# Strassen's seven products for the second expert layer's hidden units, in three blocks of tokens

## The chip, the cores and the metric

The kernel runs on one core of one Trainium2 chip. The metric is the device time of one execution in microseconds (us), as the median of several runs; the profile is a further execution with the hardware profiler on. The engines are PE (TensorE; PEld are its weight loads), DVE (VectorE), ACT (ScalarE), POOL (GpSimd) and SP (SyncE, which issues DMAs).

## The reference

Three layers follow one another. The first is an attention over 4 batches, 8 heads of 64, with 512 local tokens (a window of 32 to either side, and 32 global tokens) and 32 global ones that see everything. Its output is a matrix x of 2176 tokens by 512. Then come two expert layers:

```python
h = np.maximum(x @ w_in, 0.0)          # first layer: 512 -> 2048 -> 512
x = h * h @ w_out

logits = x @ w_gate                    # second layer: 8 experts, 512 -> 1024 -> 512
P = np.exp(logits - logits.max())
for _ in range(8):                     # Sinkhorn
    P /= P.sum(1, keepdims=True) + 1e-09
    P /= P.sum(0, keepdims=True) + 1e-09
    P *= N / E
for e in range(E):
    out += P[:, e:e + 1] * (np.maximum(x @ w1[e], 0.0) @ w2[e])
```

Everything has float32's precision; w_in and w_out arrive as float64.

## The kernel before

A product with float32's precision is made of three PE matmuls in the format float32r: each operand is held as a pair (hi, lo), and `split_terms` gives hi x hi, hi x lo and lo x hi. Making a pair takes a copy into hi (ACT or POOL) and a subtraction into lo (DVE or POOL).

The attention ends in `xh` and `xl`, the pairs of x with its 512 features in four chunks of 128 partitions and the 2176 tokens along the free axis. The expert layers then go unit by unit; a unit is 512 hidden units in four pieces of 128. The first layer has U1 = 4 units, the second 16 (two for each expert). For each unit the tokens come in five blocks of 4, 4, 3, 3 and 3 tiles of 128. For each block, `hidden` (products at L237) makes four pieces: 4 chunks x 3 terms = 12 matmuls, weights stationary, 512 or 384 tokens moving. `hidden_out` turns them into pairs; in the second layer by ACT's Relu from PSUM (L249) and a DVE subtraction that reads PSUM and the hi part (L250). Then the outputs (`products`, L860): in the second layer `second_out` has 12 matmuls for each tile of 128 tokens, hidden units stationary and 512 columns of w2 moving, and DVE adds the result, scaled by the gate's probability, to `acc` (L908).

The order of each engine's instructions is the order in which the program emits them. `step_side` and `step_gate`, called after each piece and each output, put in steps of the work beside: the weights of the next unit (loaded by SP, split by POOL for the second layer at L177 and L179, six slots of pieces), and the gate. The gate's logits come from `gate_block` (L784), with w_gate padded to 128 columns and held as pairs, during the second layer's first unit; `gate_turn` (L794) turns them. `sinkhorn` then does its eight iterations in steps, the sums over tokens by a float32 matmul with ones (L819). The first layer's result is split into `xh` and `xl` again at L878 and L879.

Of the kernel before, what the change touches and what calls it, by code (L numbers as in the profile page):

```python
# [9 lines left out]
F32 = mybir.dt.float32  # L10
# [19 lines left out]
def kernel(  # L30
# [38 lines left out]
    # tiles of the attention whose place weights take at its end  # L69
# [12 lines left out]

    def double_words(raw, k):
# [6 lines left out]
        t = cv.tile([P, 512], F32, tag=f"t{k}", name="t")  # L90
        top = cv.tile([P, 512], F32, tag=f"top{k}", name="top")
        low = cv.tile([P, 512], F32, tag=f"low{k}", name="low")
# [29 lines left out]
    U1 = F1 // (UF * P)  # L122
    UE = F2 // (UF * P)
    NU = U1 + E * UE
    # of each slot (hi, lo) of the first weights [d, (chunk, unit)] and of the second ones [unit, d]
# [12 lines left out]
    def piece_src(g):  # L138
        u, fc = divmod(g, UF)
        if u < U1:  # L140
            f0 = g * P
            return w_in.bitcast(U32)[:, 2 * f0 : 2 * (f0 + P)], w_out.bitcast(U32)[f0 : f0 + P, :]
        e, half = divmod(u - U1, UE)
        f0 = (half * UF + fc) * P
        return w1[e, :, f0 : f0 + P], w2[e, f0 : f0 + P, :]
# [3 lines left out]
    def load_part(g, part, r=None):  # L149
        if g >= NU * UF:  # L150
            return
        src = piece_src(g)[part]
        if r is None:
            r = stage.tile([P, 1024], F32, tag=f"r{part}", name="raw")
            r = r.bitcast(U32) if g < U1 * UF else r[:, 0:512]
# [9 lines left out]
    def take(g, part, k):  # L165
        """The first steps of a part of a piece, which don't need its slot."""
        if g < U1 * UF:
            taken[g, part] = yield from double_words(raw[g][part], k)

    def place(g, part, then=None):  # L170
        """The last steps, into the slot."""
        hi, lo = slots[g % NB][part]
        if g < U1 * UF:
            yield from split_words(hi, lo, *taken.pop((g, part)))
        else:
            src = raw[g][part]
            nc.gpsimd.tensor_scalar(out=hi, in0=src, scalar1=1.0, scalar2=0.0, op0=ALU.mult, op1=ALU.add)  # L177
            yield
            nc.gpsimd.tensor_tensor(out=lo, in0=src, in1=f32(hi), op=ALU.subtract)  # L179
            yield  # L180
        placed.add((g, part))
        (then or (lambda: load_part(g + 2, part)))()
# [58 lines left out]
    def hidden_out(g, ps, n, r, s, rest):  # L241
        hh, hl = (x[:, 0:n] for x in hid[g % UF])
        if g < U1 * UF:
            nc.scalar.activation(out=r, in_=ps, func=AF.Relu)  # L244
            nc.scalar.activation(out=s, in_=r, func=AF.Square)
            nc.vector.tensor_tensor(out=hh, in0=r, in1=r, op=ALU.mult)  # L246
            rest.tensor_tensor(out=hl, in0=s, in1=f32(hh), op=ALU.subtract)  # L247
        else:
            nc.scalar.activation(out=hh, in_=ps, func=AF.Relu)  # L249
            nc.vector.scalar_tensor_tensor(out=hl, in0=ps, scalar=0.0, in1=f32(hh), op0=ALU.max, op1=ALU.subtract)  # L250

    # ================= attention =================
    with ExitStack() as actx:
# [59 lines left out]
        def warm(k):  # L313
            """Products of zeros: they keep the tensor engine at its full clock until there is work without gaps."""
# [11 lines left out]
        # masks of the negated scores  # L326
# [24 lines left out]
        def evacuate(*jobs):  # L351
            """Splits of PSUM into (hi, lo) that the next step does."""
# [47 lines left out]
        def prep_edges(n):  # L400
# [8 lines left out]
            else:  # L409
                # The first block has no previous keys and the last no next ones: the mask covers what lies there.  # L410
# [10 lines left out]
        def prep_v(n):  # L421
# [9 lines left out]
            # As with the keys, the mask covers what lies beyond the ends.  # L431
# [11 lines left out]
        # global keys and queries of all batches: [2 heads x 64, (hi, lo), pair, (batch, position)]  # L443
# [8 lines left out]
        # -- local queries: half an item is a pair of heads by two blocks of 128 queries --  # L452
# [76 lines left out]
        # -- global queries: four heads of 32 queries stacked on the partitions --  # L529
# [36 lines left out]
        def glob_normalise(i):  # L566
            # The reciprocal sums wait for the products: a partition has one query here and there.
# [6 lines left out]
        def glob_transpose(i, n):  # L574
# [7 lines left out]
            # The global keys land on the partitions that vg has their values on.  # L582
# [5 lines left out]
        def glob_values(i, n):  # L588
# [6 lines left out]
            # each head's queries by the values of all four heads  # L595
# [56 lines left out]
        # Step k has the products of scores k and values k - 4 and the turning of probabilities k - 2, all of them  # L652
        # read from PSUM in the next step, where softmax k - 1 goes on too.
# [82 lines left out]
    psh = ctx.enter_context(tc.tile_pool(name="psh", bufs=3, space=PSUM))  # L736
    psy = ctx.enter_context(tc.tile_pool(name="psy", bufs=3, space=PSUM))
    psm = ctx.enter_context(tc.tile_pool(name="psm", bufs=2, space=PSUM))
# [7 lines left out]
    acc_d = acc.rearrange("p (c n) -> p c n", c=NC)  # L746
    acc_t = acc.rearrange("p (j d) -> p j d", d=DM)

# [10 lines left out]
    wg = {}  # L759
    ones = mp.tile([P, P], F32, name="ones")  # L760
    prob = mp.tile([P, NTILE, E], F32, name="prob")
    l2 = mp.tile([P, NTILE, 2 * E], F32, name="l2")
    mxb = mp.tile([P, P], F32, name="mxb")
    ss = mp.tile([P, 64], F32, name="ss")

    def gate_setup():
        wga = cv.tile([P, NC, P], F32R, tag="top0", name="wga")
        wgb = cv.tile([P, NC, P], F32R, tag="low0", name="wgb")
        wg[0] = wga, wgb
        nc.vector.memset(f32(wga), 0.0)  # L770
        nc.vector.memset(f32(wgb), 0.0)
        nc.vector.memset(ones, 1.0)
        nc.vector.tensor_copy(wga[:, :, 0:E], wgr)
        nc.vector.tensor_copy(wgb[:, :, 0:E], wgr)
        nc.vector.tensor_tensor(out=wga[:, :, E : 2 * E], in0=wgr, in1=f32(wga[:, :, 0:E]), op=ALU.subtract)

    def gate_block(tb):
        j0, nj = blocks[tb]
        c0, n = j0 * P, nj * P
        ps = psm.tile([P, 512], F32, tag="m", name="m")  # L780
        k = 0
        for c in range(NC):
            for w, x in zip(wg[0], (xh, xl)):
                nc.tensor.matmul(ps[:, 0:n], lhsT=w[:, c, :], rhs=x[:, c, c0 : c0 + n], start=(k == 0), stop=(k == 2 * NC - 1))  # L784
                k += 1
        lt = tp.tile([P, 512], F32, tag="r", name="lt")
        nc.scalar.copy(lt[0 : 2 * E, 0:n], ps[0 : 2 * E, 0:n])
        return lt

    def gate_turn(tb, lt):  # L790
        j0, nj = blocks[tb]
        ps = psm.tile([P, 4, 2 * E], F32, tag="m", name="m")
        for t in range(nj):
            nc.tensor.transpose(ps[:, t, :], lt[0 : 2 * E, t * P : (t + 1) * P], ident[0 : 2 * E, 0 : 2 * E])  # L794
        nc.scalar.copy(l2[:, j0 : j0 + nj, :], ps[:, 0:nj, :])

    def sinkhorn():
        nc.vector.tensor_tensor(out=prob, in0=l2[:, :, 0:E], in1=l2[:, :, E : 2 * E], op=ALU.add)
# [5 lines left out]
        ps = psm.tile([P, P], F32, tag="m", name="m")  # L804
# [6 lines left out]
        for _ in range(SINKHORN):  # L811
# [6 lines left out]
            ps = psm.tile([P, NTILE, E], F32, tag="m", name="m")  # L818
# [8 lines left out]

    def prepare(g):
# [157 lines left out]
```

## Time and profile before

| | |
|---|---|
| median of 3 runs | 2093.18 us (2092.74 to 2093.88) |
| span of the profiled execution | 2091.8 us |
| PE busy | 2066.2 us, 99%, 10549 matmuls |
| DVE, ACT, POOL busy | 817.5, 486.9, 467.3 us |
| mean granted TensorE clock | 0.994 of full speed |

The span runs from the first to the last instruction of the profiled execution; a run's time holds a little more than it. Busy time of an engine says how much of the span it had an instruction in work; which of its waits set the end is read from the chain of work that ended last, which is followed back from the last instruction.

### The profile page before, as it was taken

How to read it: one execution, taken by the hardware profiler on the slowest of the kernel's cores; microseconds unless marked ns; L12 is line 12 of the kernel's file. 1: busy time of each engine (PE TensorE's matmuls, PEld its weight loads, DVE VectorE, ACT ScalarE, POOL GpSimd, SP SyncE). 2: the span in 40 equal slices, each digit the busy share in tenths (PEclk: the TensorE clock that was granted, in tenths of full speed). 3: DMA queues.
4: the chain of work that ended last, by engine and by line, in shares of the span. 5: the costliest groups of instructions: out<-in, count | busy, mean ns of one | idle time of the engine just before them, and what ended most of it. 6: DMA issues, size and time to landing. Idle time of an engine off the chain costs nothing.

```text
span 2091.8 us, 26331 instructions
## 1 busy us (share of the span) xinstructions
PE 2066.2 (99%) x10549; PEld 1826.9 (87%) x10549; DVE 817.5 (39%) x1633; ACT 486.9 (23%) x1121; POOL 467.3 (22%) x567
## 2 busy tenths in 40 slices
PE   8998999999999999999999999999999999999999
PEld 7997798998989898888889898888889888888988
DVE  7999556656421343322222222222222222222222
ACT  6896442333322111101111011111111110111111
POOL 6556332315320211202020210202020220202000
PEclk8999999999999999999999999999999999999999
DMA  7664111111010101101010100101010110101011
GB/s 158 138 144 123 41 61 43 42 49 31 5 36 11 31 11 31 39 2 41 1 41 11 31 21 21 41 1 41 1 41 11 31 32 9 41 1 41 1 36 51
DMA packets 160730, 80.33 MB, mean 38 GB/s; under 512 B 95840, under 2 KB 148320, under 8 KB 160608
## 3 DMA queue, kind: packets, MB, share of 16 engines
q1 hardware_dynamic: 160608, 78.65, 14.1%
q8 instruction: 83, 1.36, 0.3%
q14 instruction: 39, 0.32, 0.1%
HBM read 63.72 MB, written 4.46 MB: 33 GB/s over the span
## 4 chain that ended last, share of the span: by engine, by line
PE 93%; DVE 4%; ACT 1%; issue 1%; DMA 1%; POOL 0%; SPq 0%; DVEq 0%; POOLq 0%; ACTq 0%
PE y L860 44%; PE h L237 44%; PE pv L524 1%; PE s L461 1%; PE pta L507 1%; DVE e L471 1%; DVE xl L363 0%; PE pv L602 0%; PE ptb L510 0%; PE s L548 0%; PE m L784 0%; DVE al L363 0%; DVE hid L246 0%; DVE bl L363 0%; DMA vb<-va 0%
## 5 line engine op out<-in xcount | busy, mean ns | idle before, releaser
L237 PE MATMUL h<-xh,w 128*128 128x384 f32 (+1 forms) x3200 | 901.6, 357 | 0.8 <-ACT rs L244 0.8
L860 PE MATMUL y<-w,hid 128*128 128x512 f32 x3276 | 755.8, 389 | 0.0
L860 PEld LDWEIGHTS y<-w,hid 128*128 128x128 f32 x3276 | 612.6, 188 | 124.7
L237 PEld LDWEIGHTS h<-xh,w 128*128 128x128 f32 x3200 | 588.4, 188 | 53.1 <-ACT rs L244 1.2
L237 PE MATMUL h<-xl,w 128*128 128x384 f32 (+1 forms) x1600 | 570.4, 356 | 0.0
L249 ACT ACTIVATE hid<-h 128x384 fp32r<-128x384 f32 (+1 forms) x320 | 171.1, 535 | 1266.7 <-PE h L237 1262.7
L250 DVE SCALAR_TENSOR_TENSOR hid<-h,hid 128x384 fp32r<-128x384 f32 (+1 forms) x320 | 195.5, 611 | 631.6 <-ACT hid L249 631.6
L908 DVE SCALAR_TENSOR_TENSOR acc<-y,prob,acc 128x512 f32<-128x512 f32 x239 | 174.3, 749 | 438.2 <-PE y L860 437.7
L177 POOL TENSOR_SCALAR w<-raw 128x512 fp32r<-128x512 f32 x128 | 81.2, 640 | 1175.3 <-PE h L237 1041.7
L237 PEld LDWEIGHTS h<-xl,w 128*128 128x128 f32 x1600 | 300.5, 188 | 26.4
L860 PE MATMUL y<-hid,w 128*128 128x384 f32 (+1 forms) x960 | 191.5, 357 | 4.4 <-DVE hid L247 2.2
L860 PEld LDWEIGHTS y<-hid,w 128*128 128x128 f32 x960 | 171.8, 188 | 21.3 <-DVE hid L247 3.4
L179 POOL TENSOR_TENSOR w<-raw,w 128x512 fp32r<-128x512 f32 x128 | 166.3, 1310 | 5.4
L113 POOL TENSOR_TENSOR top<-top,w 128x512 f32<-128x512 f32 x32 | 47.7, 1498 | 215.1 <-ACT w L111 155.6
L246 DVE TENSOR_TENSOR hid<-r 128x384 fp32r<-128x384 f32 (+1 forms) x76 | 53.8, 708 | 84.1 <-ACT r L244 84.0
L244 ACT ACTIVATE r<-h 128x384 f32<-128x384 f32 (+1 forms) x76 | 40.3, 531 | 140.9 <-PE h L237 139.4
L492 POOL TENSOR_SCALAR e<-e,st 128x224 f32<-128x224 f32 x128 | 55.5, 453 | 66.4 <-PE pta L581 26.1
L482 ACT ACTIVATE e<-e,st 128x224 f32<-128x224 f32 x128 | 60.1, 475 | 7.4 <-DVE st L471 7.3
L247 DVE TENSOR_TENSOR hid<-g,hid 128x384 fp32r<-128x384 f32 (+1 forms) x76 | 58.4, 768 | 7.9
L875 DVE TENSOR_TENSOR acc<-y,acc 128x384 f32<-128x384 f32 (+1 forms) x60 | 36.3, 608 | 49.8 <-PE y L860 49.8
L461 PE MATMUL s<-kt,q 64*128 64x224 f32 x384 | 43.4, 296 | 6.9 <-DVE st L471 2.9
L461 PEld LDWEIGHTS s<-kt,q 64*128 64x128 f32 x384 | 37.0, 195 | 12.2 <-DVE st L471 3.7
(152 smaller groups left out, 1160.6 us busy)
## 6 DMA issues: line engine op xcount, KB each, us to landing
raw<-in_moe_w_dram SPq DMA_DIRECT2D x128, 256.0 KB, 2.8
raw<-in_moe_w_in_dram SPq DMA_DIRECT2D x16, 512.0 KB, 3.8
raw<-in_moe_w_out_dram SPq DMA_DIRECT2D x16, 512.0 KB, 4.2
rqk<-in_k_l_dram SPq DMA_DIRECT2D x32, 128.0 KB, 2.6
rqk<-in_q_l_dram SPq DMA_DIRECT2D x32, 128.0 KB, 2.8
rv<-in_v_l_dram SPq DMA_DIRECT2D x32, 128.0 KB, 2.7
out_dram<-acc SPq DMA_DIRECT2D x15, 256.0 KB, 2.0
vb<-va SPq DMA_DIRECT2D x32, 112.0 KB, 3.2
```

Source lines behind the costliest of these rows:

```text
L177: nc.gpsimd.tensor_scalar(out=hi, in0=src, scalar1=1.0, scalar2=0.0, op0=ALU.mult, op1=ALU.add)
L179: nc.gpsimd.tensor_tensor(out=lo, in0=src, in1=f32(hi), op=ALU.subtract)
L237: nc.tensor.matmul(ps, lhsT=w, rhs=x, start=(k == 0), stop=(k == 3 * NC - 1))
L246: nc.vector.tensor_tensor(out=hh, in0=r, in1=r, op=ALU.mult)
L247: rest.tensor_tensor(out=hl, in0=s, in1=f32(hh), op=ALU.subtract)
L249: nc.scalar.activation(out=hh, in_=ps, func=AF.Relu)
L250: nc.vector.scalar_tensor_tensor(out=hl, in0=ps, scalar=0.0, in1=f32(hh), op0=ALU.max, op1=ALU.subtract)
L461: nc.tensor.matmul(s[:, t, :], lhsT=a, rhs=c, start=(x == 0), stop=(x == 2))
L482: nc.scalar.activation(out=v, in_=v, func=AF.Exp, bias=st[:, c : c + 1], scale=-1.0, accum_out=st[:, 4 + c : 5 + c])
L492: nc.gpsimd.tensor_scalar(out=v, in0=v, scalar1=st[:, 4 + c : 5 + c], scalar2=1.0, op0=ALU.mult, op1=ALU.mult)
L860: nc.tensor.matmul(ps, lhsT=w, rhs=m, start=(f == 0 and x == 0), stop=(f == last and x == 2))
L908: nc.vector.scalar_tensor_tensor(out=s, in0=ps, scalar=prob[:, j, e : e + 1], in1=s, op0=ALU.mult, op1=ALU.add)
```

## The change

The second layer's hidden products are done as one two-by-two block product in Strassen's form (Winograd's variant): tokens in two halves, features in two halves (A11, A12, A21, A22), and 256 hidden units in two halves of 128 (B11 to B22). Four sums of each side, S1 to S4 and T1 to T4, are made by POOL in float32 and then split into pairs; seven products of 6 matmuls each take the place of eight. The results come together partly in PSUM, where a product accumulates on another's bank, and partly by DVE additions with a copy of an intermediate result in SBUF (`snaps`).

The tokens go in three blocks TBS of 6, 6 and 5 tiles (halves of 384, 384 and 320 tokens), and the loop over them is now outside that over the 16 units: all w1 and w2 are loaded and split once per block. The forms of a block's tokens lie in `xh` and `xl`, the hidden units' pairs behind them. `step_side` no longer runs in the second layer; `hook` steps the gate and, in the outputs, four steps of the next unit's weights. The first layer's outputs stay float32 in `acc`; `gate_block` multiplies them with w_gate as plain float32, 4 matmuls of 8 columns per tile. PSUM has 2 x 2 + 1 banks for hidden products and 3 for outputs.

```diff
+    def form_sums(tb):
...
+        add = nc.gpsimd.tensor_tensor
+        add(out=s1, in0=a21, in1=a22, op=ALU.add)
+        yield
+        add(out=s2, in0=s1, in1=a11, op=ALU.subtract)
+        yield
+        add(out=s4, in0=a12, in1=s2, op=ALU.subtract)
+        yield
+        add(out=s3, in0=a11, in1=a21, op=ALU.subtract)
+        yield
+    def form_splits(tb):
...
+        for name in FORMS:
+            src = sums[tb][name]
+            hi, lo = token_form(name, n)
+            nc.scalar.copy(hi, src)
+            nc.vector.tensor_tensor(out=lo, in0=src, in1=f32(hi), op=ALU.subtract)
+            yield
+    def weight_splits(s, q, t, plain):
...
+        for c, k, src in srcs:
+            nc.scalar.copy(dst(0, c, k), src)
+            yield
+        for c, k, src in srcs:
+            nc.vector.tensor_tensor(out=dst(1, c, k), in0=src, in1=f32(dst(0, c, k)), op=ALU.subtract)
+            yield
+    def second_weights(s):
+        for q in range(2):
+            r = raw_pairs.pop((s, q, 1))
+            for i in range(2):
+                split_pool(*slots[2 * q + i][1], r[:, i])
+            load_pair_of_pieces(s + 1, q, 1)
+    PRODUCTS = {
+        1: ("A11", "B11"), 2: ("A12", "B21"), 3: ("S4", "B22"), 4: ("A22", "T4"),
+        5: ("S1", "T1"), 6: ("S2", "T2"), 7: ("S3", "T3"),
+    }
+    ORDER = ((1, 0), (5, 0), (2, 0), (1, 1), (5, 1), (6, 0), (2, 1), (6, 1), (3, 0), (7, 0), (3, 1), (7, 1), (4, 0), (4, 1))
+    def second_hidden(n, hook):
...
+        def hide(z, piece, half):
+            hh, hl = (x[:, half * n : (half + 1) * n] for x in hidden_of(piece, n))
+            nc.scalar.activation(out=hh, in_=z, func=AF.Relu)
+            late.append((z, hh, hl))
+        def flush():
+            for z, hh, hl in late:
+                nc.vector.scalar_tensor_tensor(out=hl, in0=z, scalar=0.0, in1=f32(hh), op0=ALU.max, op1=ALU.subtract)
+            late.clear()
+        def add(ps, snap, piece, half):
+            z = tp.tile([P, 512], F32, tag="rg"[count[0] % 2], name="z")[:, 0:n]
+            count[0] += 1
+            nc.vector.tensor_tensor(out=z, in0=ps, in1=snap, op=ALU.add)
+            flush()
+            hide(z, piece, half)
+        for i, q in ORDER:
+            if i == 1:
+                a[q] = psa.tile([P, 512], F32, tag="a", name="pa")[:, 0:n]
+                product(1, q, a[q], True)
+                nc.scalar.copy(p1, a[q])
...
+            elif i == 7:
+                product(7, q, a[q], False)
+                add(a[q], p5[q], 2 * q + 1, 1)
+            else:
+                product(4, q, a[q], False)
+                flush()
+                hide(a[q], 2 * q, 1)
+            hook()
+        flush()
+    for tb, (j0, nj) in enumerate(TBS):
+        n = nj * P // 2
+        for u in range(NS):
+            s = tb * NS + u
+            second_weights(s)
+            if u == NS // 2:
+                run(form_sums(tb + 1))
+            second_hidden(n, step_gate)
+            if tb == 0 and u == UE:
+                while gate:
+                    step_gate()
+            todo = []
+            if s + 1 < len(TBS) * NS:
+                todo.append(first_weights(s + 1, range(2)))
+            if u == NS - 1:
+                todo.insert(0, form_splits(tb + 1))
+            work = itertools.chain(*todo)
+            next(work, None)
+            def hook():
                 step_gate()
+                for _ in itertools.islice(work, 4):
+                    pass
...
+            for i, tile_ in enumerate(order):
+                second_out(tb, u, tile_, s == len(TBS) * NS - 1 and i == nj - 1, hook)
+            run(work)
```

`first_weights` makes the four T sums of both halves of a unit's weights (`weight_sums`, POOL, 256 elements a partition each) and then steps through `weight_splits`. In the last unit of the first layer the sums of block 0 are made on POOL, and its seven `form_splits` stand in the side work of the last `first_out`; `gate_block` for the last tokens follows it.

## Rows read from the trace of the kernel before

**Rows 1.** The page: busy time of each engine, and the granted clock in 40 slices.

```profile
PE 2066.2 (99%) x10549; PEld 1826.9 (87%) x10549; DVE 817.5 (39%) x1633; ACT 486.9 (23%) x1121; POOL 467.3 (22%) x567
...
PEclk8999999999999999999999999999999999999999
```

**Rows 2.** The page: the chain that ended last, by line.

```profile
PE y L860 44%; PE h L237 44%; PE pv L524 1%; PE s L461 1%; PE pta L507 1%; DVE e L471 1%; DVE xl L363 0%; PE pv L602 0%; PE ptb L510 0%; PE s L548 0%; PE m L784 0%; DVE al L363 0%; DVE hid L246 0%; DVE bl L363 0%; DMA vb<-va 0%
```

**Rows 3.** The chain in order of time through one unit of the second layer: start and length in us, what, and how many. Left out are the second block of 512 tokens, which is like the first, and the third of 384, which is like the second.

```profile
784.21 10.88 PE h L237 x48
795.09 10.88 PE y L860 x48
...
827.73 8.35 PE h L237 x48
836.07 8.20 PE y L860 x36
844.27 8.34 PE h L237 x48
...
877.37 2.72 PE h L237 x12
```

**Rows 4.** Busy time by stretch (PE, PEld, DVE, ACT, POOL, each with its count; granted clock, DMA share, GB/s).

```profile
784.00:2090.00 1306.00, 1304.60 (x6229) 1139.58 (x6228) 352.76 (x537) 149.68 (x280) 197.35 (x211) 1.00 0.08 24
```

**Rows 5.** PE in order of time, at 384 columns (three matmuls from 1499.72 to 1500.24) and at 256 (the values of the attention).

```profile
1499.72 0.51 PE L237 MATMUL h<-xh,w 128*128 128x384 f32 x2
...
1500.24 0.51 PE L237 MATMUL h<-xh,w 128*128 128x384 f32 x2
...
102.04 0.28 PE L524 MATMUL pv<-al,va 128*128 128x256 f32 x1
102.16 0.28 PE L524 MATMUL pv<-ah,va 128*128 128x256 f32 x1
```

**Rows 6.** The chain in order of time, the gate's pieces: a block of 512 tokens and its four turns, a block of 384 (there are two and three of them), and a sum of a Sinkhorn iteration.

```profile
596.35 1.81 PE m L784 x8
...
609.05 0.35 PE m L794 x4
...
642.10 1.39 PE m L784 x8
...
705.44 0.23 PE m L819 x2
```

**Rows 7.** Groups of instructions by line, shapes apart: count, busy us, mean ns of one, idle before.

```profile
L237 PEld LDWEIGHTS h<-xh,w 128*128 128x128 f32 x3200 | 588.4, 188 | 53.1 <-ACT rs L244 1.2
L250 DVE SCALAR_TENSOR_TENSOR hid<-h,hid 128x384 fp32r<-128x384 f32 x192 | 107.0, 557 | 334.7 <-ACT hid L249 334.7
L250 DVE SCALAR_TENSOR_TENSOR hid<-h,hid 128x512 fp32r<-128x512 f32 x128 | 88.5, 691 | 296.8 <-ACT hid L249 296.8
L875 DVE TENSOR_TENSOR acc<-y,acc 128x384 f32<-128x384 f32 x36 | 19.8, 555 | 29.1 <-PE y L860 29.1
L908 DVE SCALAR_TENSOR_TENSOR acc<-y,prob,acc 128x512 f32<-128x512 f32 x237 | 173.3, 751 | 436.6 <-PE y L860 436.0
L111 ACT CAST w<-top 128x512 fp32r<-128x512 f32 x32 | 19.0, 616 | 32.9 <-DVE top L102 19.8 <-PE y L860 13.1
```

**Rows 8.** DVE in order of time, the rows' part (4 operations from 701.33) and the columns' part (5 from 709.12) of one Sinkhorn iteration.

```profile
701.33 0.28 DVE L812 TENSOR_REDUCE ss<-prob 128x17 f32<-128x136 f32 x1
...
702.16 0.30 DVE L815 TENSOR_TENSOR prob<-prob,ss 128x136 f32<-128x136 f32 x1
...
709.12 0.29 DVE L821 TENSOR_REDUCE ss<-m 128x8 f32<-128x136 f32 x1
...
710.09 0.30 DVE L825 TENSOR_TENSOR prob<-prob,ss 128x136 f32<-128x136 f32 x1
```

**Rows 9.** In order of time, the end of a hidden piece: the first matmul of what follows on PE, and ACT's read of the piece.

```profile
2044.31 0.61 PE L860 MATMUL y<-w,hid 128*128 128x512 f32 x2
2044.51 0.60 ACT L249 ACTIVATE hid<-h 128x512 fp32r<-128x512 f32 x1 [2.12 <-PE h L237]
```

**Rows 10.** Durations of a line (minimum, median and maximum in ns; span of its starts in us; shapes), and DVE and POOL in order of time near 575 and 588 us.

```profile
L247 DVE TENSOR_TENSOR hid<-g,hid x76: 557/559/1607, 234.2 to 578.3; 128x384 fp32r<-128x384 f32 x48, 128x512 fp32r<-128x512 f32 x28
L250 DVE SCALAR_TENSOR_TENSOR hid<-h,hid x320: 550/558/693, 588.9 to 2080.8; 128x384 fp32r<-128x384 f32 x96, 128x512 fp32r<-128x512 f32 x64
...
574.58 1.46 DVE L247 TENSOR_TENSOR hid<-g,hid 128x384 fp32r<-128x384 f32 x1
576.61 0.56 DVE L247 TENSOR_TENSOR hid<-g,hid 128x384 fp32r<-128x384 f32 x1
...
574.15 1.47 POOL L179 TENSOR_TENSOR w<-raw,w 128x512 fp32r<-128x512 f32 x1
588.34 1.29 POOL L179 TENSOR_TENSOR w<-raw,w 128x512 fp32r<-128x512 f32 x1
588.86 0.69 DVE L250 SCALAR_TENSOR_TENSOR hid<-h,hid 128x512 fp32r<-128x512 f32 x1 [2.83 <-ACT hid L249]
```

**Rows 11.** Durations of POOL's lines, in the same form.

```profile
L177 POOL TENSOR_SCALAR w<-raw x128: 614/623/1172, 496.7 to 1995.3; 128x512 fp32r<-128x512 f32 x128
L179 POOL TENSOR_TENSOR w<-raw,w x128: 1281/1290/1740, 498.8 to 1996.0; 128x512 fp32r<-128x512 f32 x128
L879 POOL TENSOR_TENSOR xl<-acc,xh x20: 1010/1018/1297, 509.1 to 586.7; 128x384 fp32r<-128x384 f32 x12, 128x512 fp32r<-128x512 f32 x8
```

More of the change, by code (lines that the diff above doesn't have):

```diff
@@ L777, in gate_block @@
[L777 to L795, printed above, removed]
+    logits = []
+    def gate_block(b):
+        if not logits:
+            logits.append(psa.tile([P, NTILE, E], F32, tag="m", name="lg"))
+        for j in range(blocks[b][0], blocks[b][0] + blocks[b][1]):
+            tb = next(i for i, (j0, nj) in enumerate(TBS) if j0 <= j < j0 + nj)
+            t0 = (j - TBS[tb][0]) * P
+            for c in range(NC):
+                nc.tensor.matmul(
+                    logits[0][:, j, :], lhsT=first_outputs(tb)[:, c, t0 : t0 + P], rhs=wgr[:, c, :],
+                    start=(c == 0), stop=(c == NC - 1),
+                )
@@ L847, in hidden, with first_out @@
         hidden_out(g, ps, n, r, s, nc.vector)
-    def products(outs, n, terms):
-        tiles = [None] * len(outs)
+    def first_out(u, c0, n):
+        assert all((u * UF + i, 1) in placed for i in range(UF))
+        tiles = [None] * NC
         last = UF - 1
         order = [(0, f) for f in range(last)] + [(1, f) for f in range(last)] + [(0, last), (1, last)]
-        order += [(o, f) for o in range(2, len(outs)) for f in range(UF)]
-        for o, f in order:
+        order += [(d, f) for d in range(2, NC) for f in range(UF)]
+        for d, f in order:
@@ L882, in second_out @@
[L882 to L903 removed]
+            if f < last:
+                continue
@@ new lines, in form_splits @@
+    def form_splits(tb):
+        if tb >= len(TBS):
+            return
+        n = TBS[tb][1] * P // 2
+        for name in FORMS:
[4 more added lines that the diff above has]
+            yield
+    chunks = (
+        [slots[i][part][x] for i in (4, 5) for part in range(2) for x in range(2)],
+        [slots[i][0][x] for i in range(UF) for x in range(2)],
+    )
@@ new lines, in second_hidden, with product @@
+    def second_hidden(n, hook):
+        a, d, u2, p5 = {}, {}, {}, {}
+        p1 = snaps[:, 0, 0:n]
+        late = []
+        count = [0]
+        def product(i, q, ps, first):
+            x, w = (token_form(PRODUCTS[i][0], n), weight_form(q, PRODUCTS[i][1]))
+            t = 0
+            for k in range(2):
+                for lhs, rhs in split_terms(w[0][:, k], w[1][:, k], x[0][:, k], x[1][:, k]):
+                    nc.tensor.matmul(ps, lhsT=lhs, rhs=rhs, start=(first and t == 0), stop=(t == 5), skip_group_check=True)
+                    t += 1
+        def hide(z, piece, half):
[17 more added lines that the diff above has]
+                nc.scalar.copy(p1, a[q])
+            elif i == 5:
+                d[q] = psa.tile([P, 512], F32, tag="m", name="pd")[:, 0:n]
+                product(5, q, d[q], True)
+                p5[q] = snaps[:, 1 + q, 0:n]
+                nc.scalar.copy(p5[q], d[q])
+            elif i == 2:
+                b = psb.tile([P, 512], F32, tag="b", name="pb")[:, 0:n]
+                product(2, q, b, True)
+                add(b, p1, 2 * q, 0)
+            elif i == 6:
+                product(6, q, a[q], False)
+                u2[q] = snaps[:, 3 + q, 0:n]
+                nc.scalar.copy(u2[q], a[q])
+            elif i == 3:
+                product(3, q, d[q], False)
+                add(d[q], u2[q], 2 * q + 1, 0)
+            elif i == 7:
+                product(7, q, a[q], False)
+                add(a[q], p5[q], 2 * q + 1, 1)
+            else:
+                product(4, q, a[q], False)
[3 more added lines that the diff above has]
+        flush()
@@ new lines, in second_out @@
+    def second_out(tb, u, tile, split, hook):
+        j0, nj = TBS[tb]
+        e, half = divmod(u, UE)
+        j = j0 + tile
+        for d0, dn in ((0, DM // 2), (DM // 2, DM // 2)) if split else ((0, DM),):
+            d = slice(d0, d0 + dn)
+            ps = psy.tile([P, 512], F32, tag="y", name="y")[:, 0:dn]
+            t = 0
+            for f in range(UF):
+                hh, hl = (x[:, tile * P : (tile + 1) * P] for x in hidden_of(f, nj * P // 2))
+                wh, wl = (x[:, d] for x in slots[f][1])
+                for lhs, rhs in split_terms(hh, hl, wh, wl):
+                    nc.tensor.matmul(ps, lhsT=lhs, rhs=rhs, start=(t == 0), stop=(t == 3 * UF - 1))
+                    t += 1
+            hook()
+            s, pr = acc_t[:, j, d], prob[:, j, e : e + 1]
+            if u == 0:
+                if tb == 0:
+                    nc.scalar.copy(s, ps)
+                else:
+                    nc.scalar.activation(out=s, in_=ps, func=AF.Copy, scale=pr)
+            elif e == 0 and tb == 0:
@@ L937 @@
                 step_side(5 if opens else 2)
+                if u == U1 - 1 and tb and fc == 1:
+                    gate_block(tb - 1)
             if u == 0 and tb == 0:
@@ L941 @@
                 prepare(UF)
-            if u == U1:
-                lt = gate_block(tb)
-            if u < U1:
-                first_out(u, c0, n)
-            else:
-                second_out(u, tb, u == NU - 1 and last)
-            if u == U1:
-                gate_turn(tb, lt)
+            if u == U1 - 1 and last:
+                side.append((None, form_splits(0)))
+                step_side(2)
+            first_out(u, c0, n)
+            if u == U1 - 1 and tb == 1:
+                side.append((None, form_sums(0)))
         closed.clear()
@@ L952, with first_weights @@
             step_side(1)
-        if u == U1 + UE - 1:
-            while gate:
-                step_gate()
+    tw = share.tile([P, 2, 4, 2, P], F32, tag="va0", name="tw")
+    snaps = share.tile([P, 5, NH], F32, tag="va1", name="snaps")
+    def first_weights(s, qs):
+        for q in qs:
+            run(weight_sums(s, q, tw[:, q]))
+        for q in qs:
+            for plain in (True, False):
+                yield from weight_splits(s, q, tw[:, q], plain)
+            raw_pairs.pop((s, q, 0))
+            load_pair_of_pieces(s + 1, q, 0)
+    raw_pairs.pop((0, 0, 0))
+    load_pair_of_pieces(1, 0, 0)
+    run(first_weights(0, (1,)))
+    gate_block(len(blocks) - 1)
+    gate.append(sinkhorn())
+    NS = E * UE
+    for tb, (j0, nj) in enumerate(TBS):
+        n = nj * P // 2
[16 more added lines that the diff above has]
+            def hook():
+                step_gate()
+                for _ in itertools.islice(work, 4):
+                    pass
+            order = list(range(nj))
+            if tb == len(TBS) - 1 and u == NS - 1:
+                order = [0, 1, nj - 1, *range(2, nj - 1)]
+            for i, tile_ in enumerate(order):
+                second_out(tb, u, tile_, s == len(TBS) * NS - 1 and i == nj - 1, hook)
+            run(work)
 _INS = ['q_l', 'k_l', 'v_l', 'q_g', 'k_g', 'v_g', 'moe_w_in', 'moe_w_out', 'moe2_w_gate', 'moe2_w1', 'moe2_w2']
```

219 lines of the change are left out of this document (113 added, 106 removed).

## The prediction

> **What bounds the kernel now.** I read the page's busy shares and slices first [rows 1], then the chain that ended last [rows 2], then that chain in order of time through one unit of the second layer [rows 3]. PE is busy 99% of the span at full granted clock, and 44% of the chain is the hidden products (L237), 44% the output products (L860). In the unit from 784.21 to 877.37 us the chain is nothing but blocks of 48 and 36 matmuls end to end. So time is PE's column count, plus a fixed part per matmul, plus whatever new wait the change puts in PE's way. The other engines have room on average: between 784 and 2090 us DVE is busy 353 of 1306 us and POOL 197 [rows 4].
>
> **Part 1, seven products for eight.** What one matmul takes is read from start to start. At 512 columns it is 10.88 / 48 = 226.7 ns [rows 3], at 384 columns 0.52 / 3 = 173.3 ns, at 256 columns 120 ns [rows 5]. The three lie on one line: columns / 2.4 GHz plus 13.3 ns. The 256-column row also shows that weight loads don't bind down to 120 ns, so 320 columns are put at 133.3 + 13.3 = 146.7 ns.
>
> Before, one unit's hidden products take 2 x 10.88 + 8.35 + 2 x 8.34 = 46.79 us [rows 3]. After, a unit is done three times, each with 14 products of 6 matmuls: 84 x 173.3 ns = 14.56 us for the two blocks of six tiles (384 columns), 84 x 146.7 ns = 12.32 us for the block of five (320 columns), 41.44 us together. That is 5.35 us less for each of 16 units: **-85.6 us**. The output products stay: 17 tiles of 12 matmuls at 512 columns, 16.3 us for six tiles and 13.6 us for five. The two ends are close here: by columns alone it would be 87, by [rows 3] and the line 85.6.
>
> **Part 2, the gate.** Removed: 40 matmuls with xh and xl, 2 x 1.81 + 3 x 1.39 = 7.8 us, and 17 turns at 0.35 / 4 us, 1.5 us [rows 6]. Added: 17 tiles x 4 chunks in plain float32. The matmul with the ones (L819) is plain float32, and [rows 6] has two instructions for each of its calls, 0.23 us for both at 136 columns; so 136 instructions here, with 8 columns each. The nearest rows are 87.5 ns for one turn of 16 columns (0.35 / 4) and 115 ns for L819. I take 100 ns, 13.6 us; the far end is a weight load of 188 ns that nothing covers [rows 7], 25.6 us. Net **+4.3 us**, from +2.6 to +16.3.
>
> **Part 3, into the second layer.** The first layer's last unit used to run straight on. Now DVE must do seven form_splits of 768 elements inside the last first_out: at 0.557 us for 384 elements and 0.691 for 512 (L250, [rows 7]) 1.04 ns for each further one, so 0.95 us each, 6.7 us, with four additions of 0.55 us (L875) among them in queue order, 2.2 us. DVE comes free from the last hidden units about 2 us into first_out, so the last addition ends at about 11 us, where PE is through after 8.3 us. gate_block(4) waits for it. **+2.7 us**, from 0 (PE's other work fills it) to 6 (POOL's sums hold DVE up too).
>
> **Part 4, the sinkhorn steps.** They were one step in each hidden() and output, which come 2.7 us apart; now it is one in each product, 1.04 us apart. One iteration's nine DVE operations take 1.1 + 1.3 us [rows 8], and it has four steps, 4.2 us of products. DVE has 14 operations of 0.555 us in 14.6 us of products already, so 2.2 us in those four. 4.6 us of DVE in 4.2 us of PE, and PE's matmul with the ones stands two products behind the rows' division in PE's queue: everything behind it waits. About six of the eight iterations fall into products: some 1.3 us each, **+8 us**, from 0 to 20.
>
> **Part 5, the steady unit: DVE's burst at the end of the products.** PE's wait is product 14, which accumulates into the bank that product 12's addition reads. The products 9 to 12 all end in an addition from PSUM (0.555 us, as L875 for 384), and each addition is followed by a subtraction for the hidden unit before (0.557 us). Count from the end of product 9: its result is there 0.2 us later (the 48th matmul of a hidden unit gives way to the next at 2044.31, ACT reads at 2044.51 [rows 9]). Undisturbed, DVE ends product 12's addition at 0.2 + 3 x 1.11 + 0.555 = 4.09 us, and product 14 is due at 4 x 1.04 = 4.16 us. It just fits; with 320 columns (0.49 us an operation, 0.88 us a product) it is 0.2 + 3 x 0.98 + 0.49 = 3.63 against 3.52 us, 0.1 us late.
>
> But the subtraction changes its kind. Today's (L250) reads PSUM and takes 550 to 693 ns whatever POOL does. The new one reads two SBUF tensors, as L247 does: 557 ns at best, up to 1607 [rows 10]. The rows of time there show why: the L247 that began at 574.58 took 1.46 us beside POOL's L179 of 574.15, and the next one 0.56 us at 576.61 with no POOL operation beside it, while L250 took 0.69 us at 588.86 inside POOL's L179 of 588.34. What is POOL doing then? After each unit's last output tile it splits four w2 pieces, 4 x (0.62 + 1.29) = 7.7 us, beginning some 2 us before the tile ends; then eight weight_sums of 256 elements, 1.29 - 2 x 0.275 = 0.74 us each (the step of 0.275 per 128 elements from L879's 1.015 and L179's 1.29, [rows 11]), until about 12 us into the products, or 13 with DVE's share. The burst is from 9.4 to 13.5 us. Each subtraction then finds POOL's operation begun 0.555 us before, with 0.19 us to go: two or three such waits, and a first one of up to 0.74, put the addition 0.3 to 1.3 us behind. I take 0.45 us for each of 48 units, **+21.6 us**. Ends: 0 (the sums are over by then) and 3 x 0.74 = 2.2 us each, 106 us, if every subtraction waits for a whole operation.
>
> The Trainium skill says of this (page "SBUF — State Buffer", section "Who interferes with whom") that a DVE instruction with two SBUF inputs and a GpSimd instruction that reads SBUF exclude one another, whoever comes second being blocked until the first is through. By it every subtraction could lose a whole POOL operation, which is the far end above; the row of 574.58 agrees in kind (1.04 us of overlap with POOL's operation cost it 0.9 us).
>
> The rest of a unit is covered. w2's splits (7.7 us) are due only at the first output tile, 12 to 14 us into the unit. The weight splits, 7 x 0.69 us of DVE and 7 x 0.62 us of ACT (L111, [rows 7]), stand beside 16.3 us of output products with 6 x 0.75 us of accumulations (L908): 9.3 us of DVE and a backlog of 1 to 2. POOL's 13.6 us lie in 31 us. If that cover went, the 4.8 us of weight splits would be late for the next product 1. SP's loads, now 48 units of four transfers, run on at about 3 x 24 GB/s [rows 4]; each is asked for most of a unit before its use.
>
> **Part 6, between blocks.** Twice, form_sums puts 4 operations of 768 elements (1.84 us) into POOL's queue ahead of the sums, in the burst; and twice form_splits adds 6.7 us of DVE to an output stage, 6.7 + 4.5 + 4.8 + 2 of backlog = 18 us beside 16.3. About 1 us for each of the four: **+4 us**, from 0 to 10.
>
> **The sum.** -85.6 + 4.3 + 2.7 + 8 + 21.6 + 4 = -45.0 us. On the profiled span, 2091.8 - 45.0 = 2046.8 us. The runs' median is 2093.18, 1.4 us above that span, for what lies around it; so **2048 us**.
>
> **Rivals.** *All hidden.* If the sums are through before product 9 and the sinkhorn waits fall into slack, parts 3 to 6 cost 0 to 15 us: 2093.2 - 85.6 + 4.3 = 2012, up to 2027. For it: POOL has only 7.7 + 5.9 us of work per unit and could start early. Against it: DVE's burst leaves 0.07 us even undisturbed, and at 320 columns nothing.
>
> *Slower: the lock in the burst.* DVE's subtractions lose a whole POOL operation each in products 9 to 12, and product 14 stands still. Price 48 x 2.2 us = 106 us, so 2093.2 - 85.6 + 15 + 106 = 2129 us. It decides from (85.6 - 15) / 48 = 1.5 us a unit on. For it: L247's maximum is 1607 ns, 1.0 us above its best, and if the w2 splits (1.29 us each) slide into the burst the waits are that long. Against it: the addition between two subtractions needs no port, and POOL's operation runs out meanwhile.
>
> *A halved version.* Part 5 at about 1.1 us, with the gate's far end: -85.6 + 16 + 53 + 10 = -7, 2086 us.
>
> **Chances.** The forecast, with 2028 to 2070 as its own range, 0.60. All hidden 0.18. The halved version, 2070 to 2089, 0.09. No change to 0.2% (2089 to 2097), which is about what a measurement of this kernel tells from none, 0.03. Slower 0.10. The range from 2015 to 2083 leaves out a third of the all-hidden case, a third of the halved one, and all above: about 2 in 10. Faster: 0.60 + 0.18 + 0.09 = 0.87.
>
> **What would show it.** Right: in the chain L237's successor takes 14.56 us in 84 matmuls with 384 columns and 12.3 with 320, and the output products 16.3 and 13.6; among the waits, PE on DVE's addition once per unit near half a microsecond, in front of the last product; DVE's subtraction of hidden units with a mean well above 0.56 us and a maximum over 1 us; gate instructions near 100 ns. Wrong: PE idle between all products (an ordering of reads and writes within xh and xl that I took to be fine), weight loads that stretch the 320-column matmuls past 150 ns, or a wait for weights at product 1.

## The result and the profile after

The changed kernel takes 2040.91 us (median of 4 runs, 2036.57 to 2044.99) where the kernel before takes 2093.46 beside it: a ratio of 0.9749, 95% interval 0.9732 to 0.9766. The forecast was 2048 in a range from 2015 to 2083. The profiled run took 2037.85 us with a span of 2035.9, so 55.9 us less than the span of [rows 1]; the forecast for it was 45.0 less. The sum came near, but its terms did not: one of 21.6 us was not there, and others were missing.

The page after, which answers to [rows 1] (busy time, granted clock) and to [rows 2] (the chain by line):

```profile
PE 1997.6 (98%) x10820; PEld 1814.2 (89%) x10820; DVE 1210.8 (59%) x2398; ACT 807.9 (40%) x1856; POOL 922.6 (45%) x1071
...
PEclk8999999999989999999999999999999999999999
...
PE y L1050 36%; PE pa L987 18%; PE pd L987 9%; PE y L854 8%; PE h L246 8%; PE pb L987 5%; DVE e L476 1%; PE pv L529 1%; DVE xl L368 1%; DVE xl L997 1%; DVE al L368 1%; PE lg L783 1%; DVE z L1003 1%; DVE bl L368 1%; PE s L466 1%
```

PE is still the chain, in the seven products (L987, by the banks pa, pd and pb) and the outputs (L1050). DVE and POOL have become half busy. The slice from 560 to 611 us has a granted clock of 0.8 to 0.9, which before has nowhere past the start.

The chain in order of time, which answers to [rows 3]: a steady unit of 384 columns, the start of the next, one of 320 columns (the start of its products, and its outputs), and unit 8 of the first block.

```profile
696.15 16.36 PE y L1050 x72
712.51 1.06 PE pa L987 x6
713.58 1.04 PE pd L987 x6
...
723.98 3.12 PE pa L987 x18
727.10 16.36 PE y L1050 x72
...
1772.23 0.88 PE pa L987 x6
1773.11 0.88 PE pd L987 x6
...
1810.67 13.62 PE y L1050 x60
1836.70 13.62 PE y L1050 x60
...
874.65 0.56 DVE z L1003
875.21 1.48 DVE xl L997
...
877.80 1.65 DVE xl L997
...
879.93 1.64 DVE xl L997
...
883.09 1.75 PE pa L987 x6
884.85 17.48 PE y L1050 x72
```

Products take 1.04 and 0.88 us each, 14 of them 14.59 us (712.51 to 727.10), and the unit 30.95 (26.03 with 320 columns), without a gap. In unit 8 the chain leaves PE for DVE's subtractions (L997), three of which take 1.5 to 1.7 us in place of 0.47.

From such rows the 55.9 us come apart as follows. Units: 2 x 30.95 + 26.03 = 87.93 us for 93.16 before, 16 times, -83.7. Gate: 112 instructions in 12.2 us are 109 ns each, 136 of them 14.8 us for 9.3 before, +5.5. Clock: stretches at the lower level after gate blocks and behind unit 8, 1.6 + 1.7 + 0.8 + 2.7 + 1.1, +7.9 (the one at 621 is counted with the Sinkhorn steps). Wait for the last addition ahead of the last gate block: +1.0. Sinkhorn steps: 5.6 us in the products of unit 0 (22.82 less 14.59 and the clock's 2.7), 6.0 in those of unit 1 (20.56 less 14.59) and 0.2 for a sum in the outputs, less the eight sums of 0.23 that stood on PE's chain before [rows 6], together +10. The two units 8 and the block change: 3.0 + 1.5 + 0.4, +4.9. That is -54.4; the other 1.5 us lie in the two kernels' starts and ends.

The granted clock was the surprise. Windows of the changed kernel: busy time of PE, PEld, DVE, ACT and POOL with counts, granted clock, DMA share and GB/s.

```profile
518.00:522.00 4.00, 4.00 (x36) 3.88 (x34) 1.53 (x3) 1.23 (x2) 0.00 (x0) 0.99 0.01 2
522.00:526.00 4.00, 4.00 (x13) 3.21 (x13) 0.00 (x0) 0.00 (x0) 0.00 (x0) 0.58 0.00 0
...
586.00:590.00 4.00, 4.00 (x18) 4.00 (x18) 0.00 (x0) 0.00 (x0) 0.00 (x0) 0.60 0.00 0
...
604.00:608.00 4.00, 4.00 (x15) 4.00 (x16) 2.81 (x3) 1.62 (x3) 3.83 (x5) 0.50 0.41 131
...
620.00:624.00 4.00, 3.31 (x12) 3.31 (x13) 3.16 (x8) 1.18 (x3) 0.00 (x0) 0.61 0.01 2
```

The chain through the first of these stretches, the gate block and what follows it (start, length, what):

```profile
518.71 3.57 PE lg L783 x32
522.28 7.05 PE h L246 x24
```

From 518.7 to 522.3 PE had 32 gate instructions of 8 columns, and then stood at 1.2 GHz, half of the full clock, for some 3 us: the next 24 matmuls of 512 columns took 7.05 us where 24 x 226.7 ns are 5.44. It fell after the gate blocks before 586 and 605 too, and after PE's waits before 621 and 884. Inside the last gate block PE also waited 1.0 us. Otherwise it counts as busy through all of them, so the busy share doesn't tell.

### The profile page after: what moved, and what is told of

Read it like the earlier page. It is cut to its first block, busy times and chain, and to the rows that moved or that the text cites. A ratio compares the mean times of both kernels' runs of the same rounds, so it can differ in the third digit from the quotient of the medians.

```text
span 2035.9 us, 29259 instructions
## 1 busy us (share of the span) xinstructions
PE 1997.6 (98%) x10820; PEld 1814.2 (89%) x10820; DVE 1210.8 (59%) x2398; ACT 807.9 (40%) x1856; POOL 922.6 (45%) x1071
## 4 chain that ended last, share of the span: by engine, by line
PE 88%; DVE 8%; issue 1%; ACT 1%; DMA 1%; SPq 1%; POOL 0%; DVEq 0%; POOLq 0%; ACTq 0%
PE y L1050 36%; PE pa L987 18%; PE pd L987 9%; PE y L854 8%; PE h L246 8%; PE pb L987 5%; DVE e L476 1%; PE pv L529 1%; DVE xl L368 1%; DVE xl L997 1%; DVE al L368 1%; PE lg L783 1%; DVE z L1003 1%; DVE bl L368 1%; PE s L466 1%
## 5 line engine op out<-in xcount | busy, mean ns | idle before, releaser
L1050 PE MATMUL y<-w,xh 128*128 128x512 f32 (+1 forms) x2184 | 672.4, 389 | 0.0
L1050 PEld LDWEIGHTS y<-w,xh 128*128 128x128 f32 x2184 | 408.9, 188 | 82.4
L987 PE MATMUL pa<-xh,w 128*128 128x384 f32 (+1 forms) x1536 | 424.4, 329 | 4.2 <-DVE z L1003 4.0
L1050 PE MATMUL y<-w,xl 128*128 128x512 f32 x1092 | 425.0, 389 | 0.0
L1064 DVE SCALAR_TENSOR_TENSOR acc<-y,prob,acc 128x512 f32<-128x512 f32 (+1 forms) x250 | 187.1, 748 | 277.7 <-PE y L1050 277.7
L987 PEld LDWEIGHTS pa<-xh,w 128*128 128x128 f32 x1536 | 278.9, 188 | 9.5 <-DVE z L1003 6.2
L987 PE MATMUL pa<-xl,w 128*128 128x384 f32 (+1 forms) x768 | 251.1, 327 | 0.0
L1050 PEld LDWEIGHTS y<-w,xl 128*128 128x128 f32 x1092 | 205.3, 188 | 42.7
L987 PE MATMUL pd<-xh,w 128*128 128x384 f32 (+1 forms) x768 | 218.8, 328 | 0.0
L997 DVE SCALAR_TENSOR_TENSOR xl<-z,xh 128x384 fp32r<-128x384 f32 (+1 forms) x288 | 183.9, 639 | 3.7
L246 PE MATMUL h<-xh,w 128*128 128x384 f32 (+1 forms) x640 | 184.3, 362 | 0.8 <-ACT rs L252 0.8
L987 PEld LDWEIGHTS pa<-xl,w 128*128 128x128 f32 x768 | 144.9, 189 | 1.8
L987 PEld LDWEIGHTS pd<-xh,w 128*128 128x128 f32 x768 | 140.8, 189 | 0.0
```

The source lines that it names most:

```text
L246: nc.tensor.matmul(ps, lhsT=w, rhs=x, start=(k == 0), stop=(k == 3 * NC - 1))
L987: nc.tensor.matmul(ps, lhsT=lhs, rhs=rhs, start=(first and t == 0), stop=(t == 5), skip_group_check=True)
L997: nc.vector.scalar_tensor_tensor(out=hl, in0=z, scalar=0.0, in1=f32(hh), op0=ALU.max, op1=ALU.subtract)
L1050: nc.tensor.matmul(ps, lhsT=lhs, rhs=rhs, start=(t == 0), stop=(t == 3 * UF - 1))
L1064: nc.vector.scalar_tensor_tensor(out=s, in0=ps, scalar=pr, in1=s, op0=ALU.mult, op1=ALU.add)
```

## The experiments

All are edits of the changed kernel; the first leaves out the iterations, and the others compute what the changed kernel computes. Up to the last pair each is a single execution, and single executions of the changed kernel alone have spans from 2033.7 to 2043.2 us. So what an edit is worth is read from the stretch that it changes; the span alone doesn't show it.

**Without the iterations.**

```diff
-SINKHORN = 8
+SINKHORN = 0
```

> Leaves out the eight Sinkhorn iterations (the probabilities stay the exponentials). In the changed kernel the products of the second layer's units 0 and 1 lasted 22.8 and 20.6 us, where 14.6 is undisturbed. Theory 1, DVE's Sinkhorn steps fill the queue between two products and PE's matmul with the ones waits: units 0 and 1 come to about 17.3 (what is left is the clock that stands at half for the first products) and 14.6 us, the span falls by 12 to 15 us, to 2021 to 2024. Rival, POOL's work on the first weights at the layer's start holds DVE up through the shared port: unit 0 and 1 stay above 18 us, the span falls by under 4 us.

Measured: 2024.54 us, span 2022.8, 13.1 less than 2035.9. The products of unit 0 took 16.6 us (604.53 to 621.12, 1.6 of the 2.0 too many at the lower clock), those of unit 1 14.59. Theory 1 holds: DVE's small operations among the products, and what waits for them, cost 11 us, the matmuls with the ones included; the first weights on POOL don't. The rest of the 13.1 us is for the most part the clock, which costs the first products and the gate block ahead of them less in this execution (1.6 us for 2.7, and 0.3 for 0.8).

**Gate in single tiles.** `gate_tile` multiplies one tile (8 instructions); it is called after a hidden piece or an output of the next block, and for the last three tiles after the first three products.

```diff
-                if u == U1 - 1 and tb and fc == 1:
-                    gate_block(tb - 1)
+                if gate_tiles and fc:
+                    gate_tile()
...
-    gate_block(len(blocks) - 1)
-    gate.append(sinkhorn())
+    def gate_hook():
+        if gate_tiles:
+            gate_tile()
+            if not gate_tiles:
+                gate.append(sinkhorn())
+        step_gate()
```

> Each tile's eight gate instructions stand alone between pieces of hidden units or outputs, and those of the last three tiles between the first products. Theory 1, PE's clock falls because a run of 24 to 32 eight-column matmuls (2.6 to 3.6 us) keeps the array almost idle: no stretch under 1.0 from 518 to 612 us but for one after a real wait, the loss of about 6.6 us there (1.6 + 1.6 + 3.4) and the wait of 1 us on the last addition go, span 2027 to 2030. Rival A, the clock falls because PE waits near there: the dips stay, and the span falls by 1 us. Rival B, eight plain float32 instructions between other matmuls cost more than in a run (a switch of format each time): over 0.15 us each, span not lower.

Measured: 2029.01 us, span 2027.1, 8.8 less. No window of 4 us from 516 to 640 us has a granted clock under 1.00. The chain shows what a tile takes alone (start, length, what):

```profile
518.31 0.79 PE lg L786 x8
519.10 2.88 PE h L246 x12
521.99 0.79 PE lg L786 x8
522.78 2.88 PE h L246 x12
```

99 ns for an instruction, and the 12 matmuls of 512 columns behind it in 2.88 us both times, where 12 x 226.7 ns are 2.72. With that an instruction standing alone costs 0.12 us, for 109 ns in a run: near nothing, and not the 0.15 us or more of rival B. The clock stays up without the runs of such instructions. At 522 and 586 PE had no wait ahead of the low stretch, so there it is the run and not waiting (rival A); at 605 the wait of 1.0 us went together with the run, and the two are not told apart. The other profiles agree: in all seven of kernels with gate blocks two to four of the blocks are followed by a low stretch, and in the four with single tiles there is no low stretch from 516 to 635 us.

**form_sums out of the burst.**

```diff
-            if u == NS // 2:
-                run(form_sums(tb + 1))
...
+            if u == NS // 2:
+                todo.append(form_sums(tb + 1))
```

> form_sums of the next block (four POOL operations of 768 elements) moves from ahead of unit 8's weight sums to behind them. Theory 1, DVE's subtractions wait for POOL's long operations in the products' burst: units 8 of blocks 0 and 1 lose their 3.0 and 1.5 us and the 1.1 us of low clock behind the first, 5 us in all, span 2030 to 2031. Rival, something else of unit 8 (the cv tile, loads): the units stay 1.5 us or more above the others, the span falls by under 2 us.

Measured: 2031.36 us, span 2029.6, 6.3 less; both units 8 last 30.95 us (881.22 to 912.16, 1376.72 to 1407.67). Theory 1 holds. The rows of the changed kernel in unit 8 show the wait itself, POOL and then DVE in order of time:

```profile
875.07 1.85 POOL L902 TENSOR_TENSOR s<-s,acc 128x768 f32<-128x768 f32 x1
877.00 2.04 POOL L904 TENSOR_TENSOR s<-acc,s 128x768 f32<-128x768 f32 x1
879.01 2.15 POOL L906 TENSOR_TENSOR s<-acc 128x768 f32<-128x768 f32 x1
...
875.13 2.20 DVE L997 SCALAR_TENSOR_TENSOR xl<-z,xh 128x384 fp32r<-128x384 f32 x1
877.26 0.55 DVE L1003 TENSOR_TENSOR z<-pd,snaps 128x384 f32<-128x384 f32 x1
877.73 1.73 DVE L997 SCALAR_TENSOR_TENSOR xl<-z,xh 128x384 fp32r<-128x384 f32 x1
```

Each subtraction begins beside a POOL operation and ends 0.4 us after it, while the addition from PSUM between them, beside the same operations, has its usual 0.55. That agrees with what the Trainium skill states (page "SBUF — State Buffer", section "Who interferes with whom"): a DVE instruction with two SBUF inputs contends with a GpSimd instruction that reads SBUF, and one with at most one SBUF input, outside the 2-port modes, doesn't.

**The same lock in every unit: order of POOL's work.** Two kernels make the weight sums twice (the second time for nothing). In the first they come ahead of w2's splits, in the second behind.

```diff
-        for q in qs:
-            run(weight_sums(s, q, tw[:, q]))
+        if s == 0:
+            for q in qs:
+                run(weight_sums(s, q, tw[:, q]))
...
+            if s + 1 < len(TBS) * NS:
+                for q in (0, 1, 0, 1):
+                    run(weight_sums(s + 1, q, tw[:, q]))
             second_weights(s)
```

> In each unit POOL makes the weight sums twice and first, then the splits of w2, so that the splits' 1.3 us operations lie in the products' burst (9.4 to 13.5 us) where the 0.74 us sums lay. The 5.9 us more of POOL are not on the path by themselves. Theory 1, what a DVE subtraction loses goes by the length of the POOL operation beside it: product 14 waits 0.5 to 1 us in each of 48 units, span 2055 to 2085. Rival, DVE's burst has room whatever POOL does, and unit 8 lost its time otherwise: units stay at 30.95 and 26.03 us, span within 4 us of 2036.

> The same work as e4_long_in_burst, but the splits of w2 come first and the doubled weight sums behind them, so that the burst has 0.74 us operations again, for all of its length. Theory 1, the length of POOL's operation decides: units of 384 columns return from 31.43 to 30.95 us, span 2034 to 2042. Rival, the additional 5.9 us of POOL is what cost e4 its time: units of 384 columns stay near 31.4 us, span over 2060.

Measured: 2089.47 us with the sums first (span 2087.7), 2035.15 with the splits first (span 2033.4). With the sums first a unit of 384 columns lasts 31.43 us, 0.48 more, and the chain goes through DVE's burst in it:

```profile
755.47 0.47 DVE xl L997
755.94 0.47 DVE z L1003
756.40 1.10 DVE xl L997
757.50 0.48 DVE z L1003
757.98 0.04 issue
758.03 1.33 PE pa L987 x6
759.36 16.36 PE y L1050 x72
```

With the splits first a unit is back at 30.95, with as much POOL work and more of it in the burst. So the length of POOL's operation decides: at 384 columns 0.74 us costs nothing, 0.62 and 1.29 us in turn cost 0.48, 1.57 us cost 1.5 (unit 8 of the second block, whose sums are for the smaller third block) and 1.84 us cost 3.0 (unit 8 of the first). But 0.48 is a little under the 0.5 to 1 expected, and most of this kernel's 51.8 us are of another kind: the first two blocks lost 16.9 us (the outputs of block 1's last unit begin at 1616.51, not 1599.65), the third 35. There POOL's sums and splits, in one row ahead of the first output, make up 19 us of a unit's 30 on the chain:

```profile
1728.50 0.94 POOL tw L942
1729.44 0.60 POOL w L80
...
1730.12 1.49 POOL w L81
```

"Not on the path by themselves" was wrong for units of 26 us in that order: sums wait until the unit's splits have read them, w2's splits wait for the sums, and outputs for those. The 16.9 us are the test of the burst; the total is not.

**Sinkhorn steps after the first eight products only.**

```diff
-            hook()
+            if k < 8:
+                hook()
```

> The gate is stepped after the first 8 products of a unit only, so none of the Sinkhorn steps stands in DVE's burst; the steps reach into unit 2. Theory 1, what costs is DVE's queue in the burst (7 of its 14 operations lie in products 9 to 14): the 5.6 and 6.0 us that units 0 and 1 lose beside the clock come to half, span 2029 to 2033. Rival, PE's matmul with the ones, two products behind, is what waits, wherever the step stands: as many iterations stand among products, span within 2 us of 2036.

Measured: 2037.49 us, span 2035.5. By the span the rival holds. From the first product to unit 2's outputs it took 90.0 us (607.29 to 697.30), where the changed kernel took 90.9 (605.21 to 696.15). But this profile has one low stretch more among these products (at 688), so the steps' place is worth more than the 0.9 us. In the kernel with three edits below, against the one with the gate in single tiles alone, the same stretch is 2.3 us shorter (87.7 for 90.0, with one low stretch in either). Some 2 us of 11, then: not the half of theory 1, and not quite nothing. The chain in unit 2 shows where the iteration stands now:

```profile
683.30 1.12 DVE ss L815
...
684.44 0.79 DVE prob L816
...
686.24 0.60 DVE prob L806
...
686.89 0.50 PE m L810 x2
```

and POOL, in order of time:

```profile
683.08 1.30 POOL L81 TENSOR_TENSOR w<-raw,w 128x512 fp32r<-128x512 f32 x1
```

L815 multiplies 8 columns and takes 1.12 us, where it takes 0.17 undisturbed (L824 before, the median). It ends within 0.05 us of the end of the split of w2 that POOL began just before it, so it waits for that one. The run below with the steps in the outputs bears this out. There the same operation takes 0.17 us three times while POOL is idle (617.9 to 633.2), and 1.11 us at 634.14, beside a split that POOL began at 633.93. PE's matmul with the ones waits for the chain of them, and the products behind it.

**All three edits together, and then the steps in the outputs.**

> Gate spread, form_sums moved and early steps together. If the three costs are separate places, the gains add: 8.8 + 6.3 + what e6_early_steps gains (0 to 6), span 2015 to 2021. Rival, the waits hand over to one another (the first weights' sums on POOL already stand in the chain once the gate is spread): 2022 to 2027.

> As e7_all, but the Sinkhorn steps stand in the outputs only, four after each tile (one iteration), and none among products; in e7_all DVE's short operations took up to 1.1 us beside POOL's splits of w2. Theory 1, the iterations cost where POOL works and where PE's next matmul is only two products behind: with POOL idle and 2.7 us between the steps, units 0, 1 and 2 have products of 14.6 to 16 us, span 2010 to 2016. Rival, DVE has 2.4 us of Sinkhorn, 1.4 of weight splits and 0.7 of accumulation in each 2.7 us of a tile: the outputs of units 0 and 1 stretch by what the products gain, span 2018 to 2024.

The three together: 2021.9 us, span 2020.1, 15.8 less, nearly the sum 8.8 + 6.3 + 0.4. The places are separate. At the layer's start the chain does pass to POOL's first weight sums, but what PE loses at the end of that is a wait of 1.0 us. With the steps in the outputs (four after each tile, none among products) it is 2025.06, span 2023.1: the products of unit 1 come to 15.8 us, but the outputs of unit 0, 16.4 undisturbed, take 22.3 (616.56 to 638.83), since DVE has 4.5 us to do in each 2.7 us of a tile. The rival holds there too: DVE's 2.4 us for an iteration have to lie beside little else, and both places are taken.

**The best version and the changed kernel, timed together.**

> The kernel of e7_all again, timed. Median 2019 to 2025 us, 0.9 to 1.2% under the changed kernel; if the dips of the granted clock after blocks of gate instructions are what spreads the changed kernel's times (2036.6 to 2045.0), this one, without such blocks, spreads by less than 4 us.

> The changed kernel unchanged, timed in the same job. Median 2037 to 2044 us; its runs spread by 5 us or more, and the longer ones have the lower mean granted clock (0.987 against 0.992).

The three edits together: 2021.97 us, 2021.51 to 2022.52 in 5 runs, a ratio of 0.9657 to the kernel before (0.9644 to 0.967). The changed kernel: 2037.18, 2035.49 to 2040.32 in 4 runs, 0.9732 (0.9718 to 0.9745). So 15 us more are to be had, and the version beats both. The spread is 1.0 us without blocks of gate instructions and 4.8 with them (a little under the 5 expected); the longest run had the lowest clock, 0.988 against 0.990 and 0.991. This second profile of the changed kernel has no low stretch at 522, the first one has: whether the clock falls after a block differs from one execution to the next.

## Why the prediction was right, and where its sum was not

The gain was forecast 10.9 us too small (45.0 for 55.9 on the profiled span). Parts 1 and 5, the units, made it 19.7 us too small (83.7 measured, 64.0 forecast), and 7.9 us of low clock, which no part had, took some of that back. Without the low clock the forecast would have been off by 18.8 us, so that the sum came as near as it did is partly luck.

*What bounds it, and part 1.* Right. 320 columns take 146.7 ns as the line said (0.88 us for six), and the products and outputs are as long as worked out. Units gain 83.7 us where -85.6 + 21.6 were forecast for them.

*Part 5, the burst.* This term was mis-sized: 21.6 us, and the trace has about 1.6. At 384 columns the last three products take 3.12 us, three times 1.04, so product 14 waits for nothing. At 320 they take 2.73 us, where three times 0.88 are 2.64: 0.1 us in each of 16 units. Its sign, PE on DVE's addition for near half a microsecond in every unit, did not come. The mechanism is there, as unit 8 and the pair of kernels show; the slip was in the base. The step "0.2 + 3 x 1.11 + 0.555 = 4.09" put DVE's durations end to end. DVE starts the next operation before one's recorded end: in a steady unit

```profile
752.95 0.56 DVE L1003 TENSOR_TENSOR z<-pd,snaps 128x384 f32<-128x384 f32 x1 [0.81 <-PE pd L987]
753.42 0.55 DVE L997 SCALAR_TENSOR_TENSOR xl<-z,xh 128x384 fp32r<-128x384 f32 x1
753.92 0.56 DVE L1003 TENSOR_TENSOR z<-pa,snaps 128x384 f32<-128x384 f32 x1
754.39 0.60 DVE L997 SCALAR_TENSOR_TENSOR xl<-z,xh 128x384 fp32r<-128x384 f32 x1
754.96 0.56 DVE L1003 TENSOR_TENSOR z<-pd,snaps 128x384 f32<-128x384 f32 x1
```

a subtraction starts 0.47 us after its addition, and where nothing holds DVE up an addition starts 0.47 us after the subtraction (755.47 and 755.94 in the rows of the kernel with the sums first). So the two need 0.94 us, beside products of 1.04. That leaves 0.1 us in each product, and POOL's sums of 0.74 us take no more than that: the subtractions beside them last 0.55 to 0.60 us, and POOL waits for DVE as often (its sums go up to 1.06 us). The first wait, which the forecast put at up to 0.74 us, is 0.25 us (the subtraction of 751.34 lasts 0.80) and falls into the 0.81 us in which DVE has nothing to do ahead of the addition of 752.95. At 320 columns the room is smaller, and the additions come 0.95 us apart beside products of 0.88:

```profile
1807.10 0.49 DVE L1003 TENSOR_TENSOR z<-pa,snaps 128x320 f32<-128x320 f32 x1
1807.50 0.62 DVE L997 SCALAR_TENSOR_TENSOR xl<-z,xh 128x320 fp32r<-128x320 f32 x1
1808.05 0.48 DVE L1003 TENSOR_TENSOR z<-pd,snaps 128x320 f32<-128x320 f32 x1
```

The near-zero end of the range was the right one. [Rows 5] were read from start to start, these were not.

*Part 2, the gate.* 109 ns an instruction for 100 forecast, +5.5 for +4.3. What it did to the clock was not in the forecast at all: 1.6 + 1.7 + 2.7 + 0.8 us in the gate blocks and behind them, with a further 1.1 behind unit 8.

*Part 3.* The wait for the last addition is 1.0 us, 2.7 forecast. DVE's splits and additions take 8.2 us (594.20 to 602.40) for 8.9 counted, and PE has six gate instructions, 0.9 us, to do ahead of the wait.

*Part 4.* Right in its place, 10 us for 8. Its reason was half: DVE's queue and PE's wait two products behind, yes, but the single operations are also longer beside POOL's, six times their length at the most, which the forecast applied to the subtractions only.

*Part 6.* 4.9 us beside the clock, for 4. Of its four places only the two form_sums cost much.

*Rivals.* "All hidden" (2012 to 2027) was the right picture of the steady units, with the steps at the layer's start against it; the kernel with three edits, at 2022, is that case. The slower rival's price is confirmed in kind by unit 8 (3.0 us with operations of 1.84 us), but the sums aren't long enough.

## What to carry to other kernels

An engine's burst is added up from start to start in the trace of the same kind of instructions; durations end to end made a pair of 0.94 us look like 1.11, and with that a slack of 10% like a loss. Where DVE reads two SBUF tensors, or makes many small steps, keep POOL's long operations out of that stretch: same work in another order cost 0.48 us a unit or nothing. Plain float32 matmuls of a few columns are put one tile at a time between full ones, and a product that replaces others is looked at for the clock behind it.

## What the runs showed that was not expected

A run of 24 to 32 matmuls of 8 columns, through which PE counts as busy, is followed by some 3 us at 1.2 GHz in some executions and not in others; eight such matmuls at a time, with full ones between them, were followed by none. A DVE operation on 8 columns took 1.12 us in place of 0.17 beside POOL's w2 splits. And a DVE operation of 0.555 us recorded length is followed by the next one 0.47 us after its start.
